# Attention with a gated spatial MLP on one core: f32 scores by 128 queries of one head with the two heads in row halves of the array, the last spatial block as two products, and new numbers for the plan

## Chip, core and metric

One NeuronCore of a Trainium2 chip runs the whole kernel. The metric is the device time of one execution in microseconds (us), median of the runs. Engine names: PE is the matrix engine, PEld its weight loads, DVE, ACT and POOL the three elementwise engines, SP the queue that issues the DMAs. A tile name like `ps` stands for any of its numbered buffers.

## What is computed

```python
def _attn_ref(q, k, v):                       # (4 batches, 12 heads, 448, 64)
    scores = scale * np.matmul(q, k.transpose(0, 1, 3, 2))
    scores = np.where(np.triu(ones, k=1), -1000000000.0, scores)
    scores = scores - np.max(scores, axis=-1, keepdims=True)
    attn = np.exp(scores)
    attn = attn / (np.sum(attn, axis=-1, keepdims=True) + 1e-09)
    return np.matmul(attn, v)
...
def _moe_ref(x, w_in, w_spatial, b_spatial, w_out):   # x: (4, 448, 768)
    h = np.maximum(x @ w_in, 0.0)                     # 768 -> 1024
    u, v = h[..., :512], h[..., 512:]
    v_n = (v - mean(v)) / np.sqrt(var(v) + 1e-06)
    v_s = np.einsum('ts,bsd->btd', w_spatial, v_n) + b_spatial[None, :, None]
    return (u * v_s) @ w_out                          # 512 -> 768
```

## The kernel before

The 48 heads are worked on as 24 pairs (6 to a batch). A pair goes through load of q and k, `qk_turn` or `qk_prepare` (transposed q and k in `qkT`), `attend` (scores, mask and maximum, exponential, division, transposed weights in `et`, product with v in `px`) and ends in `xT`, one sixth of a batch's feature rows split in an f16 high and low part. After a batch's pairs `ffn(b)` makes four groups of chained products in three PSUM banks `pf`: the v half (`wi` streamed, `xT` as weights), the u half (`xT` streamed), the spatial product (`wst` streamed, the normalised `vn` as weights) and the output (`wo` streamed, `g` and `gt` as weights). An f16 product is three matmuls, high by high, high by low, low by high (`TERMS`).

Pairs are treated in three ways. `SINGLE` (0 to 14): scores are one f32 product each. 64 queries of both heads stand as one block-diagonal weight tile (`q32`, 128 rows by 128 columns: head 0 in rows 0 to 63, head 1 in 64 to 127, zeros elsewhere), and k of both heads streams past it (`k32`); a unit `c` covers queries 64c to 64c+63 and streams 64(c+1) columns, seven units to a pair, two in a bank (`BANKS`). An f32 matmul stands in the trace as two records with a weight load each. The remaining pairs have their scores as f16 high and low products in column halves of the array (L746, L747) from q and k that DMAs transpose. `TURNED` (0 to 8): the weights after the softmax stay f32 and PE transposes them (L807), and the product with v (L893) is f32, one head in each column half of the array. The other pairs split them in f16 high and low and let DMAs transpose them.

Order: every function only adds operations with engines, estimated costs and dependencies to a `Plan`. `assign` spreads the free ones over ACT, DVE and POOL; `run` plays the estimates forward and fixes each engine's order and the buffers. `TUNE`, `SLACK`, `EARLY`, `SPLITS`, `LAZY` and the costs therefore decide where an operation stands, not what it does. For the four `ffn` groups and the pairs that means that PE's queue mixes chains of three (`pf`, L1118) with pieces of attention. Lines of the profile that are used: L578 transposes of q and k, L736 f32 scores, L746/L747 f16 scores, L757 mask and maximum, L769 exponential, L782/L790 division, L427/L459 and L438 high and low parts, L893 product with v, L1118 all `ffn` chains.

## Time and profile before

| | |
|---|---|
| median of 3 runs (range) | 406.49 us (405.89 to 406.72) |
| the profiled execution | 406.36 us, span 404.6 us |
| busy: PE, DVE, ACT, POOL | 371.9, 280.7, 259.2, 198.1 us |
| PE idle | 32.7 us of the span |

The span runs from the first to the last instruction; 1.8 us of the execution lie around it. Busy PE counts pipelined matmuls, so the price of a piece of PE work is read below from the start of one group to the start of the next one on a full queue, not from the length of its records.

### The profile page before, as it was taken

Reading aid. Unit: us, or ns where it says so; the run is one execution under the profiler, and the core shown is the slowest. Engines: PE = TensorE matmul, PEld = TensorE weight load, DVE = VectorE, ACT = ScalarE, POOL = GpSimd, SP = SyncE. Lnnn points to the kernel's source line nnn. Section 1 sums busy time; section 2 is a strip of 40 time slices with the busy share of each in tenths; the row PEclk is TensorE's granted clock in tenths of the full one; section 3 lists DMA queues with packets and bytes.
Section 4 is the critical chain, followed back from the end, with each engine's and each line's share of the span. In section 5 each row is a group of like instructions: output and inputs, shape, how many; then the busy total and the mean of one; then the engine's idle time right before and its main releaser. Section 6 shows DMA issues by size and latency. Waiting matters only on the chain. (4 is left out here: it accounts for less than half of the span.)

```text
span 404.6 us, 7631 instructions
## 1 busy us (share of the span) xinstructions
PE 371.9 (92%) x2438; PEld 231.4 (57%) x2438; DVE 280.7 (69%) x955; ACT 259.2 (64%) x744; POOL 198.1 (49%) x276
## 2 busy tenths in 40 slices
PE   5578869997999999999999999999996999999995
PEld 4455444663556466865545459855452568445595
DVE  4366868889767997977887898676996884031211
ACT  3779867688977566997867957666763655123120
POOL 2310489566887665006289387525892340054120
PEclk9899998999999999999999999999996999999999
DMA  8974882346193349997979978998775546400013
GB/s 176 235 154 145 222 170 101 105 95 148 43 219 87 118 123 172 172 226 174 192 161 206 169 135 191 190 208 197 128 137 105 98 87 120 129 2 0 0 48 109
DMA packets 156298, 55.60 MB, mean 137 GB/s; under 512 B 150177, under 2 KB 152034, under 8 KB 156258
## 3 DMA queue, kind: packets, MB, share of 16 engines
q1 hardware_dynamic: 156258, 55.12, 65.0%
q8 instruction: 19, 0.31, 0.3%
q14 instruction: 21, 0.17, 0.1%
HBM read 26.76 MB, written 5.51 MB: 80 GB/s over the span
## 5 line engine op out<-in xcount | busy, mean ns | idle before, releaser
L736 PE MATMUL ps<-qkT 128*128 128x64 f32 (+6 forms) x210 | 61.7, 422 | 6.8 <-ACT et L827 3.4
L769 ACT ACTIVATE ps<-ps,sm 128x384 f32<-128x384 f32 (+4 forms) x105 | 48.7, 464 | 29.6 <-DVE sm L757 21.6
L1118 PE MATMUL pf<-xT,wi 128*128 128x448 f16 x288 | 62.9, 356 | 0.2 <-ACT u L1265 0.2
L1118 PE MATMUL pf<-wi,xT 128*128 128x512 f16 (+1 forms) x360 | 62.3, 340 | 0.0
L1118 PE MATMUL pf<-wo,g 128*128 128x384 f32 x288 | 59.3, 351 | 0.2 <-DVE u L1291 0.2
L857 DVE SCALAR_TENSOR_TENSOR e<-ps,sm,e 128x256 f16<-128x256 f32 (+4 forms) x105 | 49.4, 504 | 9.4 <-ACT e L425 8.7
L427 POOL TENSOR_SCALAR e<-e,sm 128x64 f32<-128x64 f32 (+6 forms) x51 | 31.1, 626 | 49.4 <-DVE sm L790 33.8
L757 DVE CUSTOM_DVE_ANT_0 ps<-ps,mask 128x384 f32<-128x384 f32 (+6 forms) x105 | 44.1, 443 | 15.5 <-PE ps L736 14.7
L425 ACT ACTIVATE e<-ps,sm 128x384 f16<-128x384 f32 (+4 forms) x105 | 46.2, 507 | 13.3 <-DVE sm L790 9.5
L1118 PEld LDWEIGHTS pf<-wo,g 128*128 128x128 f32 x288 | 49.7, 188 | 4.6 <-issue 2.7
L1118 PE MATMUL pf<-wst,vn 128*128 128x448 f16 (+1 forms) x192 | 42.8, 364 | 4.4 <-ACT u L1265 3.8
L1118 PEld LDWEIGHTS <-xT 128*128 128x128 f16 (+1 forms) x360 | 26.4, 103 | 32.6 <-issue 11.9
L736 PEld LDWEIGHTS ps<-qkT 128*128 128x128 f32 x210 | 33.0, 199 | 16.3 <-ACT et L827 5.1
L1118 PEld LDWEIGHTS <-wi 128*128 128x128 f16 x288 | 26.0, 98 | 27.4 <-issue 7.5
L782 DVE TENSOR_SCALAR sm<-sm 128x2 f32<-128x2 f32 x96 | 24.1, 263 | 20.1 <-ACT e L769 10.4
L769 ACT ACTIVATE e<-ps,sm 128x384 f32<-128x384 f32 (+6 forms) x63 | 29.2, 476 | 11.7 <-DVE sm L757 10.0
L757 DVE CUSTOM_DVE_ANT_0 ps<-ps,mask,sc 128x384 f32<-128x384 f32 (+4 forms) x63 | 30.8, 504 | 4.4 <-PE ps L747 3.7
L427 POOL TENSOR_SCALAR vs<-vnat,vsc 128x512 f16<-128x512 f32 x15 | 10.5, 701 | 45.7 <-PE px L893 41.1
L1118 PEld LDWEIGHTS <-vn 128*128 128x128 f16 (+1 forms) x192 | 18.5, 100 | 23.7 <-issue 9.5
L807 PE MATMUL ps<-ident,e 128*128 128x128 f32 x144 | 22.1, 286 | 8.6 <-POOL e L427 5.2
L1211 POOL TENSOR_TENSOR ln<-ln,mhalf 128x1 f32<-128x1 f32 (+1 forms) x16 | 9.2, 581 | 36.7 <-DVE ln L1203 36.7
L807 PEld LDWEIGHTS ps<-ident,e 128*128 128x128 f32 x144 | 16.7, 145 | 17.2 <-POOL e L427 9.3
(122 smaller groups left out, 699.1 us busy)
## 6 DMA issues: line engine op xcount, KB each, us to landing
wb<-in_moe_w_in_dram SPq DMA_DIRECT2D x12, 512.0 KB, 4.0
vnat<-in_v_dram SPq DMA_DIRECT2D x24, 192.0 KB, 3.7
out_dram<-o SPq DMA_DIRECT2D x12, 384.0 KB, 3.3
qk<-in_q_dram SPq DMA_DIRECT2D x30, 112.0 KB, 3.7
qk<-in_k_dram SPq DMA_DIRECT2D x30, 112.0 KB, 3.7
o<-in_moe_w_out_dram SPq DMA_DIRECT2D x8, 384.0 KB, 3.4
qk<-in_q_dram SPq DMA_DIRECT2D x9, 224.0 KB, 3.8
qk<-in_k_dram SPq DMA_DIRECT2D x9, 224.0 KB, 4.3
```

The lines of the kernel that those rows point to most:

```text
L425: nc.scalar.activation(out=dst, in_=src, func=AF.Copy, scale=scale)
L427: nc.gpsimd.tensor_scalar(out=dst, in0=src, scalar1=scale, scalar2=1.0, op0=ALU.mult, op1=ALU.mult)
L736: nc.tensor.matmul(out=at(ps)[:, o0:o0 + n], lhsT=q32(t)[:, c, :], rhs=k32(t)[:, :n], start=True, stop=True)
L757: lambda e, ps=ps, n=n, u=u, sm=sm, o0=o0, m0=m0: nc.vector.tensor_tensor_reduce(out=at(ps)[:, o0:o0 + n], in0=at(ps)[:, o0:o0 + n], in1=m ...
L769: nc.scalar.activation(out=dst, in_=src, func=AF.Exp, scale=-1.0, bias=at(sm)[:, u:u + 1], accum_out=at(sm)[:, 4 + u:5 + u],)
L782: lambda e, n=n, sm=sm, esc=esc: nc.vector.tensor_scalar(out=at(sm)[:, 8:8 + n], in0=at(sm)[:, 4:4 + n], scalar1=1.0 / esc, scalar2=1e-9 / ...
L807: nc.tensor.transpose(out=at(pt)[:, 128 * i:128 * i + 128], in_=e32(at(eb))[:, E0[c] + j, :], identity=ident)
L857: lambda e, part=part, src=src, sm=sm, u=u: nc.vector.scalar_tensor_tensor(out=part(1), in0=src(), scalar=at(sm)[:, 8 + u:9 + u], in1=part(0),
L1118: nc.tensor.matmul(out=o, lhsT=a(), rhs=rhs, start=(n0 + n == 0), stop=(n0 + n == len(mms) - 1), skip_group_check=len(out_ap()) > 1,)
L1211: lambda e, ln=ln, tn=tn: nc.gpsimd.tensor_tensor(out=at(ln)[:tn, 8:9], in0=at(ln)[:tn, 8:9], in1=mhalf[:tn], op=ALU.pow),
```

## The change

1. Pairs that are both `TURNED` and `SINGLE` (now 0 to 9) are `WIDE`. A product takes 128 queries of one head: weights 64 rows by 128 columns, head 0 in rows 0 to 63, head 1 in rows 64 to 127 (`flat32`), and the two heads' products follow each other into different PSUM banks. Queries 0 to 127 stream 128 columns, 128 to 255 stream 256, 256 to 383 stream 384. The last 64 queries of both heads go to one bank, head 0 in partitions 0 to 63, head 1 in 64 to 127, each streaming 448. Three PE operations make a pair: `both(0)`, `both(2)`, `last()`. Mask, exponential, division and transposes follow the new grouping (`mask2`; five score banks to a pair where there were four, three groups of divisions where there were four).
2. `TURNED` gains pair 9; `SINGLE` loses pairs 12 to 14, which are now split and transposed like 15 to 23.
3. In the spatial product the last block of 64 tokens has its high part in rows 0 to 63 and its low part in rows 64 to 127, so that one matmul makes high by high and low by high. A second one makes high by low and the bias (`wst` and `vn3` are laid out for it, with one more copy per batch). Twelve matmuls of a chain become eleven.
4. The plan's numbers are new, so all engines' orders are.

```diff
 LAZY = 13750
 CALM = 5
-SPLITS = 1, 6
-EARLY = 20570
+SPLITS = 2, 7
+EARLY = 14463
 WAYS = "qkw"
 
-TURNED = frozenset(range(9))
-
-SINGLE = frozenset(range(15))
-SLACK = 345.0, 270.0, 0.0, 100.0, 412.0, 440.0
-TUNE = 23000.0, 5468.0, 44064.0, 3408.0, 785.0, 805.0, 3458.0, 21900.0, 6260.0, 15846.0
+TURNED = frozenset(range(10))
+
+SINGLE = frozenset(range(12))
+SLACK = 393.0, 184.0, 100.0, 40.0, 677.0, 440.0
+TUNE = 33297.0, 2734.0, 63857.0, 6028.0, 898.0, 884.0, 3458.0, 18815.0, 8564.0, 15846.0
 
 
 class Buf:
@@ -307,6 +308,8 @@
...
+
+    WIDE = [t and w for t, w in zip(TURNS, WHOLE)]
...
+
+    mask2 = phys["e"][0][:, 17 * 128:21 * 128]
...
-    store("sm", 3, [128, 16], F32)
+    store("sm", 6, [128, 16], F32)
...
-        if any(WHOLE):
-            for t in phys["qkT"]:
-                nc.vector.memset(q32(t), 0.0)
...
         t = s["qkT"] = Buf("qkT")
+        if not WIDE[p]:
...
-            parts = [(slice(0, 64), 0), (slice(64, 128), 64)] if n == 0 else [(slice(0, 128), None)]
+            parts = [(slice(0, 64), 0), (slice(64, 128), 64)] if n == 0 and not WIDE[p] else [(slice(0, 128), None)]
...
 
+
+
+    GROUPS = [
+        [(0, 0, 128, 0, 0), (0, 128, 256, 128, 1)],
+        [(1, 0, 128, 0, 3), (1, 128, 256, 128, 4)],
+        [(0, 256, 384, 0, 6)],
+        [(1, 256, 384, 0, 9)],
+        [(None, 384, S, 0, 12)],
+    ]
+    HR = 1408
+
+    def wide(p, eb, et):
+
+
+        s, rank = st[p], 100 * p
+        banks = [Buf("ps") for _ in GROUPS]
+
+        def product(h, q0, n, bank, o0, r0, rn):
+            t = at(s["qkT"])
+            rows = slice(64 * h, 64 * h + 64)
+            nc.tensor.matmul(
+                out=at(bank)[r0:r0 + rn, o0:o0 + n], lhsT=flat32(t)[rows, q0:q0 + rn], rhs=k32(t)[rows, :n],
+                start=True, stop=True, skip_group_check=True,
...
+        def both(g):
+            for i in range(len(GROUPS[g])):
+                for h in range(2):
+                    _, q0, n, o0, _ = GROUPS[g + h][i]
+                    product(h, q0, n, banks[g + h], o0, 0, 128)
+
+        def last():
+            for h in range(2):
+                product(h, 384, S, banks[4], 0, 64 * h, 64)
+
+        sums = [Buf("sm") for _ in range(3)]
+        whose = [(sums[g // 2], 2 * (g % 2) if g < 2 else g % 2) for g in range(5)]
+        for n, fn in enumerate((lambda e: both(0), lambda e: both(2), lambda e: last())):
+            parts = [(banks[g], u) for g in (2 * n, 2 * n + 1) if g < 5 for u in range(len(GROUPS[g]))]
+            plan.add({"PE": WIDE_PE[n]}, fn, s["qkT_keys"], parts + [(eb, "room")], rank)
...
+        for g, (ps, group) in enumerate(zip(banks, GROUPS)):
+            sm, u0 = whose[g]
+            for u, (h, q0, n, o0, _) in enumerate(group):
+                plan.add(
+                    {"DVE": c_dve(n) + 8},
+                    lambda e, ps=ps, n=n, u=u0 + u, sm=sm, o0=o0, h=h: nc.vector.tensor_tensor_reduce(
+                        out=at(ps)[:, o0:o0 + n], in0=at(ps)[:, o0:o0 + n],
+                        in1=mask[:, 0:n] if h is None else mask2[:, 512 - n:512],
+                        scale=-0.125, scalar=3.0e38, op0=ALU.add, op1=ALU.min, accum_out=at(sm)[:, u:u + 1],
+                    ),
+                    [const_key("mask")], [(ps, u), (sm, f"m{u0 + u}")], rank,
+                )
...
+        for n, sm in enumerate(sums):
+            m = (4, 2, 1)[n]
+            plan.add(
+                {"DVE": 250},
+                lambda e, m=m, sm=sm: nc.vector.tensor_scalar(
+                    out=at(sm)[:, 8:8 + m], in0=at(sm)[:, 4:4 + m], scalar1=1.0, scalar2=1e-9, op0=ALU.mult, op1=ALU.add,
+                ),
+                [(sm, f"s{u}") for u in range(m)], [(sm, "d")], rank,
+            )
...
+            def turn(e, pt=pt, c0=c0, cn=cn):
+                for i in range(cn):
+                    nc.tensor.transpose(
+                        out=at(pt)[:, 128 * i:128 * i + 128], in_=e32(at(eb))[:, c0 + i, :], identity=ident
+                    )
+
+            plan.add(
+                {"PE": cn * 116}, turn, [(eb, x[4]) for x in group] + [(eb, "pad"), const_key("ident")], [(pt, 0)],
+                rank, 200,
+            )
...
+            for i in range(2 if g < 2 else 1):
+
+                def copy(e, pt=pt, i=i, g=g):
+                    by_head = at(et).rearrange("p (h r) -> p h r", h=2)
+                    blocks = at(pt)[:, 0:384].rearrange("p (j r) -> p j r", r=128)
+                    if g < 2:
+
+                        src, dst = at(pt)[:, 0:256], by_head[:, g, 0:256]
+                        if i:
+                            src, dst = at(pt)[:, 256:384], by_head[:, g, 448:576]
+                    elif g < 4:
+                        src = blocks
+                        dst = by_head[:, g - 2, 256:256 + 960].rearrange("p (j r) -> p j r", r=320)[:, :, 0:128]
+                    else:
+                        src = at(pt).rearrange("p (j h r) -> p j h r", j=4, h=2)
+                        dst = by_head[:, :, 128:HR].rearrange("p h (j r) -> p j h r", r=320)[:, :, :, 256:320]
...
-        for g, units in enumerate(BANKS):
+        if WIDE[p]:
+            wide(p, eb, et)
+        for g, units in enumerate(() if WIDE[p] else BANKS):
...
+                            if WIDE[p]:
+                                rhs = at(et)[:kk, 1408 * h + 448 * j:1408 * h + 320 * j + S]
...
+            {"POOL": c_pool(S), "ACT": c_act(S)},
+            lambda e: scaled_copy(e, wst[64:128, 0, 3, :], wst[0:64, 0, 3, :], 1.0), [], [const_key("wst", 0)], rank + 2,
+        )
...
+            for plane in range(1 if t < 3 else 2):
+                plan.add(
+                    {"ACT": c_act(512), "POOL": c_pool(512), "DVE": c_fast(512)},
+                    lambda e, hv=hv, nb=nb, tn=tn, plane=plane: scaled_copy(e, at(nb)[:tn, plane], at(hv)[:tn], 1.0),
+                    [(hv, 0)], [(nb, "h" if not plane else "hh")], -1,
+                )
...
-                    out=at(nb)[:tn, 1], in0=at(hv)[:tn], in1=at(nb)[:tn, 0], op=ALU.subtract
+                    out=at(nb)[:tn, 1] if tn == 128 else at(nb)[64:128, 0], in0=at(hv)[:tn], in1=at(nb)[:tn, 0],
+                    op=ALU.subtract
                 ),
...
-                    for j, kk in enumerate((128, 128, 128, 65)) for a, w in TERMS
+                    for j in range(3) for kk in (128,) for a, w in TERMS
+                ] + [
+                    (
+                        lambda a=a, f=f, kk=kk: at(vn[3])[:kk, a, 128 * f:128 * f + 128],
+                        lambda a=a, kk=kk: [wst[:kk, a, 3, :]], [(vn[3], x) for x in xs] + [const_key("wst", a)],
+                    )
+                    for a, kk, xs in ((0, 128, "hl"), (1, 97, ("hh",)))
                 ],
```

PE around a pair's f32 scores, before (pair 8; `ps` score banks, `e` softmax weights, `pf` an ffn chain):

```order
L807 MATMUL ps1_73<-ident_64,e1_93 128x128 x4
L736 MATMUL ps2_74<-qkT0_84 128x64
L736 MATMUL ps2_74<-qkT0_84 128x384
L807 MATMUL ps3_75<-ident_64,e1_93 128x128 x4
L807 MATMUL ps1_73<-ident_64,e0_92 128x128 x4
L1118 LDWEIGHTS vn1_115
L1118 MATMUL pf2_79<-wst_65,vn1_115 128x448
```

PE around a pair's f32 scores, after (pair 9):

```order
L754 MATMUL ps0_72<-qkT1_85 128x128
L754 MATMUL ps2_74<-qkT1_85 128x128
L754 MATMUL ps0_72<-qkT1_85 128x256
L754 MATMUL ps2_74<-qkT1_85 128x256
L1288 LDWEIGHTS wi_63
L1288 MATMUL pf1_78<-xT4_100,wi_63 128x448
L1288 LDWEIGHTS wi_63
L1288 MATMUL pf1_78<-xT4_100,wi_63 128x448
L1288 LDWEIGHTS wi_63
L1288 MATMUL pf1_78<-xT4_100,wi_63 128x448
L754 MATMUL ps1_73<-qkT1_85 128x384
L754 MATMUL ps3_75<-qkT1_85 128x384
```

The scores of a pair still stand in pieces among chains of three; a piece is now two or four matmuls with 64 weight rows, and matmuls with 128 rows stand before and behind it. Counted over the whole of PE's order, the array's tile shape (rows by columns of weights) differs from one matmul to the next at 155 places before and at 210 after; 53 of these have a wide product on one side.

PE at the end of a spatial chain of batch 0, before:

```order
L736 MATMUL ps1_73<-qkT1_85 128x256 x2
L1118 LDWEIGHTS vn3_66
L1118 MATMUL pf2_79<-wst_65,vn3_66 128x448
L1118 LDWEIGHTS vn3_66
L1118 MATMUL pf2_79<-wst_65,vn3_66 128x448
L1118 LDWEIGHTS vn3_66
L1118 MATMUL pf2_79<-wst_65,vn3_66 128x448
```

and after:

```order
L1288 LDWEIGHTS wi_63
L1288 MATMUL pf2_79<-xT5_101,wi_63 128x448
L1288 LDWEIGHTS vn3_66
L1288 MATMUL pf1_78<-wst_65,vn3_66 128x448
L1288 LDWEIGHTS vn3_66
L1288 MATMUL pf1_78<-wst_65,vn3_66 128x448
L1288 LDWEIGHTS wi_63
```

The block `vn3` has two matmuls where it had three.

POOL between the normalisation of batch 2 and its gates, before (`qk` and `qks` are the high and low parts of a pair's q and k, `vs` those of its v):

```order
L427 TENSOR_SCALAR vn3_66<-hv1_113 64x512
L427 TENSOR_SCALAR qk2_82<-qk2_82,sc2_122 112x512
L1242 TENSOR_TENSOR vn3_66<-hv1_113,vn3_66 64x512
L427 TENSOR_SCALAR qk2_82<-qk2_82,sc2_122 112x512
L427 TENSOR_SCALAR qks0_83<-qk2_82 112x8x64 x2
L459 TENSOR_TENSOR qks0_83<-qk2_82,qks0_83 112x8x64 x2
L427 TENSOR_SCALAR vs0_90<-vnat1_87,vsc1_126 128x8x64
L427 TENSOR_SCALAR vs1_91<-vnat1_87,vsc1_126 128x8x64
L427 TENSOR_SCALAR g0_105<-u0_104 128x384
```

and after:

```order
L1413 TENSOR_TENSOR vn2_116<-hv0_112,vn2_116 128x512
L1413 TENSOR_TENSOR vn3_66<-hv1_113,vn3_66 64x512
L436 TENSOR_SCALAR vn3_66<-hv1_113 64x512
L436 TENSOR_SCALAR vs1_91<-vnat1_87,vsc1_129 128x8x64
L436 TENSOR_SCALAR qk2_82<-qk2_82,sc2_125 112x512 x2
L436 TENSOR_SCALAR qks0_83<-qk2_82 112x8x64 x2
L468 TENSOR_TENSOR qks0_83<-qk2_82,qks0_83 112x8x64 x2
L436 TENSOR_SCALAR g0_105<-u0_104 128x384
```

The run of six operations on `qk2` and `qks` stands there again, now wholly behind `vn3` and with `vs1` ahead of it. On DVE the subtraction for `vs` stands right behind the scale of that same pair in both orders.

## Rows read from the trace of the kernel before

**Rows 1.** The page: span, then busy time, share and instructions of each engine.

```profile
span 404.6 us, 7631 instructions
PE 371.9 (92%) x2438; PEld 231.4 (57%) x2438; DVE 280.7 (69%) x955; ACT 259.2 (64%) x744; POOL 198.1 (49%) x276
```

**Rows 2.** Four stretches: busy time of PE, PEld, DVE, ACT, POOL; granted clock, DMA share, GB/s.

```profile
0.00:62.00 62.00, 43.93 (x238) 28.56 (x238) 37.24 (x154) 45.53 (x135) 21.82 (x50) 0.97 0.83 180
62.00:304.00 242.00, 235.65 (x1618) 144.00 (x1618) 204.18 (x690) 178.83 (x526) 151.09 (x195) 0.99 0.75 155
304.00:314.00 10.00, 6.24 (x25) 2.14 (x23) 6.51 (x17) 4.02 (x10) 2.02 (x3) 0.66 0.54 96
314.00:400.30 86.30, 86.09 (x564) 56.67 (x562) 32.74 (x96) 30.33 (x74) 23.19 (x30) 1.00 0.28 65
```

**Rows 3.** Timeline of PE, 115 to 146 us: start, length, group, count.

```profile
115.17 2.10 PE L893 MATMUL px<-et,vnat 128*64 128x448 f32 x16
117.20 1.89 PE L736 MATMUL ps<-qkT 128*128 128x192 f32 x8
...
128.13 1.03 PE L736 MATMUL ps<-qkT 128*128 128x64 f32 x4
129.00 1.04 PE L807 MATMUL ps<-ident,e 128*128 128x128 f32 x8
129.88 0.73 PE L1118 MATMUL pf<-wst,vn 128*128 128x448 f16 x3
...
139.74 0.92 PE L736 MATMUL ps<-qkT 128*128 128x448 f32 x2
140.50 3.57 PE L1118 MATMUL pf<-wst,vn 128*128 128x448 f16 x18
143.90 0.55 PE L578 MATMUL ps<-ident,qk 112*128 112x112 f32 x4
144.29 1.87 PE L1118 MATMUL pf<-wst,vn 65*128 65x448 f16 x9
```

**Rows 4.** Timeline of PE, 105 to 107 us: half and full array in turn.

```profile
105.28 0.52 PE L1118 MATMUL pf<-wi,xT 128*64 128x256 f16 x6
105.73 0.74 PE L1118 MATMUL pf<-xT,wi 128*128 128x448 f16 x3
106.40 0.52 PE L1118 MATMUL pf<-wi,xT 128*64 128x256 f16 x6
```

**Rows 5.** Timeline of PE, 252 to 257 us: f16 product with v, then f16 scores.

```profile
252.01 1.62 PE L893 MATMUL px<-et,vs 128*64 128x448 f16 x24
253.56 0.28 PE L746 MATMUL ps<-qkT 128*64 128x192 f16 x2
...
255.00 0.80 PE L1118 MATMUL pf<-wo,g 128*128 128x384 f32 x3
255.73 0.38 PE L746 MATMUL ps<-qkT 128*64 128x448 f16 x2
...
256.23 2.87 PE L1118 MATMUL pf<-wo,g 128*128 128x384 f32 x15
```

**Rows 6.** The chain that ended last, from 300 us: start, length, what.

```profile
300.54 1.42 DVE sc L479
301.97 4.59 DVE vs L438
...
307.47 0.64 ACT u L1265
...
308.15 4.64 PE pf L1118 x12
```

**Rows 7.** Timeline of POOL beside it.

```profile
301.26 0.68 POOL L427 TENSOR_SCALAR qk<-qk,sc 112x512 f32<-112x512 f32 x1
...
305.33 0.69 POOL L427 TENSOR_SCALAR vs<-vnat,vsc 128x512 f16<-128x512 f32 x1
```

**Rows 8.** The group of that DVE line: count, busy us, mean ns, idle before.

```profile
L438 DVE SCALAR_TENSOR_TENSOR vs<-vnat,vsc,vs 128x512 f16<-128x512 f32 x15 | 16.3, 1086 | 0.5 <-POOL vs L427 0.4
```

More of the change, by code (lines that the diff above doesn't have):

```diff
@@ L341, in q32, with flat32 @@
         return t.bitcast(F32)[:, 0:2 * S].rearrange("p (c r) -> p c r", r=128)
+    def flat32(t):
+        return t.bitcast(F32)[:, 0:S]
     def k32(t):
@@ L528, in constants @@
         nc.gpsimd.memset(mask[:, S:512], NEG)
+        nc.gpsimd.memset(mask2[:, 0:384], 0.0)
+        nc.gpsimd.memset(mask2[:, 384:512], 0.0)
+        nc.gpsimd.affine_select(
+            out=mask2[:, 384:512], in_=mask2[:, 384:512], pattern=[[-1, 128]], compare_op=ALU.is_ge, fill=NEG,
+            base=0, channel_multiplier=1,
+        )
         for t in phys["e"]:
@@ L565, in load @@
             )
+    blank = {}
     def qk_turn(p):
@@ L571, in qk_turn, with clear @@
         t = s["qkT"] = Buf("qkT")
+        if not WIDE[p]:
+            def clear(e):
+                if not blank.get(at(t).name):
+                    nc.gpsimd.memset(q32(at(t)), 0.0)
+                    blank[at(t).name] = True
+            plan.add({"POOL": 300}, clear, [], [(t, (0, 0)), (t, (0, 1))], rank)
         for n in range(2):
@@ L585, in qk_turn, with copy @@
             )
-            parts = [(slice(0, 64), 0), (slice(64, 128), 64)] if n == 0 else [(slice(0, 128), None)]
+            parts = [(slice(0, 64), 0), (slice(64, 128), 64)] if n == 0 and not WIDE[p] else [(slice(0, 128), None)]
             for i, (rows, c0) in enumerate(parts):
-                def copy(e, pt=pt, rows=rows, c0=c0):
+                def copy(e, pt=pt, rows=rows, c0=c0, n=n):
                     src = at(pt)[rows, :S]
                     if c0 is None:
-                        dst = k32(at(t))
+                        dst = k32(at(t)) if n else flat32(at(t))
+                        if not n:
+                            blank[at(t).name] = False
                     else:
@@ L700, with even @@
     held = {}
+    GROUPS = [
[41 more added lines that the diff above has]
+                )
+            for u, (_, _, n, o0, c) in enumerate(group):
+                plan.add(
+                    {"ACT": c_act(n, "P", 2)},
+                    lambda e, ps=ps, n=n, u=u0 + u, sm=sm, o0=o0, c=c: nc.scalar.activation(
+                        out=at(eb)[:, 128 * c:128 * c + n], in_=at(ps)[:, o0:o0 + n], func=AF.Exp, scale=-1.0,
+                        bias=at(sm)[:, u:u + 1], accum_out=at(sm)[:, 4 + u:5 + u],
+                    ),
+                    [(sm, f"m{u0 + v}") for v in range(len(group))], [(ps, u), (sm, f"s{u0 + u}"), (eb, c)], rank,
+                )
[5 more added lines that the diff above has]
+                    out=at(sm)[:, 8:8 + m], in0=at(sm)[:, 4:4 + m], scalar1=1.0, scalar2=1e-9, op0=ALU.mult, op1=ALU.add,
+                ),
+                [(sm, f"s{u}") for u in range(m)], [(sm, "d")], rank,
+            )
+            plan.add(
+                {"DVE": 150},
+                lambda e, m=m, sm=sm: nc.vector.reciprocal(out=at(sm)[:, 8:8 + m], in_=at(sm)[:, 8:8 + m]),
+                [], [(sm, "d")], rank,
+            )
+        for g, group in enumerate(GROUPS):
+            sm, u0 = whose[g]
+            for u, (_, _, n, _, c) in enumerate(group, u0):
+                def even(e, c=c, u=u, sm=sm, n=n):
+                    w = at(eb)[:, 128 * c:128 * c + n]
+                    scaled_copy(e, w, w, at(sm)[:, 8 + u:9 + u])
+                plan.add(
+                    {"POOL": 260 + 1.25 * n, "ACT": c_act(n, "S", 1), "DVE": c_fast(n, 1)}, even, [(sm, "d")],
+                    [(eb, c)], rank,
+                )
+            pt = Buf("ps")
+            c0, cn = group[0][4], 4 if g == 4 else 3
+            def turn(e, pt=pt, c0=c0, cn=cn):
+                for i in range(cn):
+                    nc.tensor.transpose(
+                        out=at(pt)[:, 128 * i:128 * i + 128], in_=e32(at(eb))[:, c0 + i, :], identity=ident
+                    )
+            plan.add(
+                {"PE": cn * 116}, turn, [(eb, x[4]) for x in group] + [(eb, "pad"), const_key("ident")], [(pt, 0)],
+                rank, 200,
+            )
+            for i in range(2 if g < 2 else 1):
[12 more added lines that the diff above has]
+                        dst = by_head[:, :, 128:HR].rearrange("p h (j r) -> p j h r", r=320)[:, :, :, 256:320]
+                    if e == "ACT":
+                        nc.scalar.activation(out=dst, in_=src, func=AF.Copy)
+                    else:
+                        nc.vector.tensor_copy(out=dst, in_=src)
+                n = (256, 128)[i] if g < 2 else 128 * cn
+                plan.add({"ACT": c_act(n, "P"), "DVE": c_dve(n)}, copy, [(pt, 0)], [(et, (g, i))], rank)
@@ L862, in attend @@
                 )
-        if turns:
+        if WIDE[p]:
+            et_keys = [(et, (g, i)) for g in range(5) for i in ((0, 1) if g < 2 else (0,))]
+        elif turns:
             et_keys = [(et, (g, i)) for g in range(4) for i in ((0, 1) if g == 1 else (0,))]
```

44 lines of the change are left out of this document (26 added, 18 removed).

## Prediction

> **What bounds the kernel now.** I read the page first, then busy time by stretches, then PE's timeline, last the chain that ended last. The page says that PE is busy 371.9 of 404.6 us and no other engine more than 280.7 [rows 1]. The stretches say where the 32.7 us of idle PE lie: 18.1 in the first 62 us, 6.3 in the next 242, 3.8 in the 10 us from 304, 0.2 in the 86 after that, and 4.3 behind PE's last matmul [rows 1, 2]. So from 62 us on PE has a full queue but for one hole, and what leaves its queue there shortens the kernel, while in the first 62 us PE waits for the other engines and work taken from it mostly becomes idle time. DVE is next, 84 % busy from 62 to 304 us, ACT 74 %, POOL 62 % [rows 2]. The chain shows what the hole is: a subtraction for `vs` on DVE that holds the chain 4.59 us, then an ACT evacuation, then PE starts again at 308.15 [rows 6].
>
> **Prices on PE.** Start to start on a full queue: 18 matmuls of 448 f16 columns take 3.40 us, 0.189 each, 0.42 ns a column [rows 3]. The f32 unit of 448 columns takes 0.76 us (139.74 to 140.50), 1.70 ns a column, four passes of the f16 price; the units of 64 and 384 together 0.87 (128.13 to 129.00), 0.11 above their columns, so a short unit pays a floor [rows 3]. A pair of 0 to 8 has 1792 columns: 0.87 + 0.76 + 896 × 1.70 ns = 3.15 us. For pairs 9 to 14 the program widens odd units, 1920 columns, 3.37 us.
>
> The f32 product with v puts one head into each column half. Its 2 × 1024 columns would take 3.48 us one after the other; they take 2.03 (115.17 to 117.20), so halves of the array do run side by side in f32, at 1.74 plus 0.29 [rows 3]. That is column halves; no row shows row halves.
>
> What entering and leaving a half costs is read where six half matmuls of 256 f16 columns alternate with three full ones: 0.45 and 0.67 us [rows 4]. Two at a time, six would take 0.32; three full ones take 0.57. That leaves 0.23 for two changes, 0.115 each.
>
> **The change, term by term.**
> 1. *Scores in row halves.* A head streams 128 + 256, then 384, then 448 columns; side by side 1216 × 1.70 ns = 2.06 us a pair, one after the other 4.13. I take 2.06: the product with v is the nearest row, f32 in halves of the same array. Nine pairs gain 1.09 each and pair 9 gains 1.31: −11.1 us. The weight loads of the first operation are not known; a transpose shows 0.11 us per 128 columns of f32 weights (eight in 0.88, 129.00 to 129.88 [rows 3]), and eight loads that don't overlap would be 0.88 where the columns take 0.65. That is 0 to +2.3 us over ten pairs; I take 0 and keep the rest for the range.
> 2. *Changes of shape.* 210 instead of 155 in PE's order: 55 × 0.115 = +6.3 us. This eats more than half of term 1, because the pieces stand among full-array chains.
> 3. *Pairs 12 to 14 in f16.* Such a pair takes 1.44 + 0.50 us with its way out and 0.115 in [rows 5], 2.05 instead of 3.37: −4.0. Their 24 transposes of q and k go, four in 0.39 us (143.90 to 144.29 [rows 3]): −2.3. Three small sums come, no dearer than a transpose: +0.3.
> 4. *Pair 9 by PE.* Sixteen transposes at 0.11: +1.8. The product with v is 2.03 us in f32 instead of 1.55 in f16 (252.01 to 253.56) [rows 3, 5]: +0.5.
> 5. *Spatial block.* Sixteen matmuls fewer at 0.189: −3.0.
> 6. *Other engines and DMAs.* Counted in the order, DVE has 20 instructions fewer, ACT 9 more, POOL 36 more. Their cover is the idle 16, 26 and 38 % of the second stretch [rows 2]; a microsecond more on ACT is paid by nobody. DMAs: three transposes and six local copies come for pairs 12 to 14, their q and k come in six loads instead of twelve, three transposes of pair 9's weights go; SP issues as many as before, and the DMA share of 0.75 [rows 2] is its cover. Without cover a pair would wait for its `qkT`; I take nothing.
>
> Terms 1 to 5: −11.1 + 6.3 − 4.0 − 2.3 + 0.3 + 2.3 − 3.0 = −11.5 us of PE work.
>
> 7. *Early pairs.* Pairs 0 to 3 are scored before 62 us. Their net gain, 1.09 less about 0.63 for changes of shape, I don't count: +1.8.
> 8. *The hole at 304 us.* DVE's subtraction starts behind the 1.42 us of L479 and lasts until POOL's six operations on `qk`, `qks` and `vs`, back to back from 301.26 to 306.02, are over [rows 6, 7]; DVE is queued, ACT's evacuation behind it, PE behind that. The loss is 3.8 us idle, and a granted clock of 0.66 (1.2 GHz for two thirds of the window, the rest at 2.4) after the pause [rows 2]; about 6.5 us together. In the changed order POOL's run and DVE's subtraction stand as close as before. But the 15 such subtractions average 1.09 us [rows 8], so mostly they don't meet a run. Between 0 and 6.5 I credit half: −3.3.
>
> Sum: −11.5 + 1.8 − 3.3 = −13.0 on the span, 404.6 to 391.6, 393.4 us with the 1.8 around it. The profiled execution is 0.1 under the median of the three runs, so **393.5 us**.
>
> A rule of the Trainium skill speaks against term 1: TensorEngine Tiling (Array Packing), Gotcha 1: PSUM Pressure, says that different row tiles cannot use one PSUM bank at a time. `last()` writes one bank from both row halves. In the product with v two halves write one bank at once without paying for it [rows 3], but those are column halves; by the rule the sum would come out as in rival B.
>
> **Rivals.**
> A. *The hole stays, or moves.* New order, same neighbours on POOL and DVE. If it costs the whole 6.5, the time is 396.8; with a second one of its size, 403.3. For it: POOL gets busier by three pairs' high and low parts, six operations each, nearly 5 us (five take 4.07 in the run of [rows 7]). Against it: one such hole in 400 us so far.
> B. *`last()` runs one head after the other.* Ten times 0.76: +7.6, 401.1 us. For it, only the shared bank; against it, that its two heads also lie in different columns of the array, as in the product with v.
> C. *Row halves don't run side by side at all* (the other sign). A pair then takes 4.13 us, 2.07 more: ten pairs +20.7, and +12.4 if the four early ones stay hidden: 406 to 414, I say 411. It decides from about 3.4 us a pair, where the 13.0 are used up. For it: no row shows row halves, and f32 takes two records and two loads for each product. Against it: column halves do it in f32.
> D. *More than the sum.* The hole goes wholly (−3.3) and the early gain counts (−1.8): 388.4.
>
> On C the skill's page TensorE: Matmul & The Clock Gate, Part 3, states that matmuls in distinct row groups run concurrently (4 row strips measured at 3.07 times the speed); no row here shows it, and by it the sum is that of term 1.
>
> **How the numbers follow.** A run here tells about 0.2 % from no change, 0.8 us. Chances: forecast 48 %, A 23 %, B 8 %, C 9 %, D 12 %. The range 387 to 402 us leaves out C, the end of A with two holes and the far end of D, about 2 in 10; it holds the 2.3 us of weight loads. The likeliest case by itself reaches from 390 to 396.5. Faster: all but C and a sliver of A, 0.89; within 0.2 %: 0.02; slower: 0.09.
>
> **What will show it.** In the timeline of the changed kernel: `last()` at 0.76 us and `both(2)` at 0.65, start to start, plus about 0.1 at either end (B would show 1.5 for the first, C 1.3 for the second too); eleven matmuls in a spatial chain at 0.189; PE busy near 360 us; L746/L747's successors for 12 pairs; and in the stretches no 10 us at a clock of 0.66. The forecast is wrong if a change of shape costs an f32 product with fresh weights much more than 0.115 us, if the first 62 us lengthen because the new order starts the weights' preparation later, or if DVE, at 84 %, becomes what PE waits for.

## The result and the profile after

| | before | after |
|---|---|---|
| median (range) | 406.61 us (405.89 to 406.88, 4 runs) | 391.76 us (389.81 to 393.82, 4 runs) |
| the profiled execution, span | 406.36, 404.6 us | 389.81, 388.1 us |
| PE busy, PE idle | 371.9, 32.7 us | 359.0, 29.1 us |

The ratio is 0.9651, 95 % interval 0.9615 to 0.9687. The runs of after spread over 1 %, four times as far as those of before; the profiled execution is the fastest of the four. Executions over 1.5 % above the fastest of their kernel are left out below (three of ten of the kernel with all pairs in the same rows, two of six of that with the early four, one of six of that with pairs 12 to 14 in f32), but for one kernel whose six runs are all told.

The page of after, the lines that answer to [rows 1]:

```profile
span 388.1 us, 7762 instructions
PE 359.0 (93%) x2474; PEld 216.7 (56%) x2474; DVE 276.5 (71%) x935; ACT 252.1 (65%) x759; POOL 225.2 (58%) x312
```

The stretches of after, columns as in [rows 2]: PE, PEld, DVE, ACT, POOL, granted clock, DMA share, GB/s.

```profile
0.00:62.00 62.00, 49.80 (x301) 27.80 (x301) 39.23 (x162) 50.94 (x164) 27.73 (x62) 0.97 0.83 187
62.00:290.00 228.00, 215.98 (x1561) 128.43 (x1561) 195.57 (x646) 164.48 (x500) 166.62 (x213) 0.99 0.79 163
290.00:300.00 10.00, 10.00 (x64) 5.04 (x64) 8.55 (x31) 6.52 (x21) 7.45 (x9) 1.00 0.63 123
300.00:384.00 84.00, 83.26 (x554) 55.41 (x550) 33.12 (x99) 29.94 (x77) 23.39 (x30) 1.00 0.33 75
```

PE's idle time is 12.2 us in the first 62 us (18.1 before), 12.0 in the next 228 (6.3 before in the 242 us up to the hole), none around 300 us, 0.7 until 384 and 4.1 behind PE's last matmul. So the hole is gone, the beginning is fuller, and the middle has become emptier.

The timeline of PE in after, the pieces of a wide pair (L754) and what follows each:

```profile
112.22 0.97 PE L754 MATMUL ps<-qkT 64*64 64x448 f32 x4
113.11 0.55 PE L826 MATMUL ps<-ident,e 128*128 128x128 f32 x3
...
117.56 0.93 PE L754 MATMUL ps<-qkT 64*128 64x128 f32 x8
118.42 0.74 PE L1288 MATMUL pf<-xT,wi 128*128 128x448 f16 x3
119.09 0.92 PE L754 MATMUL ps<-qkT 64*128 64x384 f32 x4
119.94 1.88 PE L1288 MATMUL pf<-xT,wi 128*128 128x448 f16 x9
121.96 0.97 PE L754 MATMUL ps<-qkT 64*64 64x448 f32 x4
122.86 1.14 PE L898 MATMUL ps<-qkT 128*128 128x64 f32 x4
```

Start to start `both(0)` takes 0.86 us, `both(2)` 0.85, `last()` 0.89 and 0.90: 2.60 us a pair, its changes of shape included, where the block-diagonal tile took 3.15.

The subtractions for `vs` on DVE in after (count, then min/median/max in ns), to be read against [rows 8]:

```profile
L447 DVE SCALAR_TENSOR_TENSOR vs<-vnat,vsc,vs x14: 741/744/1196, 84.3 to 317.2; 128x512 f16<-128x512 f32 x14
```

None of the 14 is stretched beyond 1.2 us, where one of 15 took 4.69 (4.59 of it in the chain of [rows 6]).

### The profile page after: what moved, and what is told of

It reads as the page before. It is cut to its first block, busy times and chain, and to the rows that moved or that the text cites. A ratio compares the mean times of both kernels' runs of the same rounds, so it can differ in the third digit from the quotient of the medians.

```text
span 388.1 us, 7762 instructions
## 1 busy us (share of the span) xinstructions
PE 359.0 (93%) x2474; PEld 216.7 (56%) x2474; DVE 276.5 (71%) x935; ACT 252.1 (65%) x759; POOL 225.2 (58%) x312
## 5 line engine op out<-in xcount | busy, mean ns | idle before, releaser
L436 POOL TENSOR_SCALAR e<-e,sm 128x128 f32<-128x128 f32 (+3 forms) x54 | 31.3, 595 | 35.6 <-DVE sm L806 21.1
L1288 PEld LDWEIGHTS <-xT 128*128 128x128 f16 (+1 forms) x360 | 26.1, 103 | 31.1 <-issue 11.5
L434 ACT ACTIVATE e<-ps,sm 128x384 f16<-128x384 f32 (+4 forms) x98 | 41.0, 520 | 3.6 <-DVE sm L952 3.6
L919 DVE CUSTOM_DVE_ANT_0 ps<-ps,mask,sc 128x256 f32<-128x256 f32 (+4 forms) x84 | 39.0, 506 | 4.6 <-PE ps L909 4.2
L789 ACT ACTIVATE e<-ps,sm 128x128 f32<-128x128 f32 (+3 forms) x70 | 34.3, 503 | 7.2 <-DVE sm L779 5.0
L754 PE MATMUL ps<-qkT 64*128 64x128 f32 (+3 forms) x160 | 30.4, 459 | 4.0 <-ACT e L789 3.2
L779 DVE CUSTOM_DVE_ANT_0 ps<-ps,e 128x256 f32<-128x256 f32 (+2 forms) x60 | 24.1, 442 | 7.1 <-PE ps L754 6.7
L468 POOL TENSOR_TENSOR qks<-qk,qks 112x512 f16<-112x512 f32 x24 | 29.1, 1229 | 0.0
L851 ACT ACTIVATE et<-ps 128x256 f32<-128x256 f32 (+3 forms) x64 | 23.4, 437 | 5.3 <-PE ps L826 3.6
L1288 PEld LDWEIGHTS <-vn 128*128 128x128 f16 (+1 forms) x176 | 16.5, 99 | 17.7 <-issue 4.5
L436 POOL TENSOR_SCALAR qk<-qk,sc 112x512 f32<-112x512 f32 x24 | 16.9, 715 | 15.5 <-ACT ps L931 8.7
L1059 PE MATMUL px<-et,vs 128*64 128x448 f16 (+3 forms) x336 | 22.7, 276 | 2.6 <-DMA et<-e 1.5
```

The costliest lines, as they stand in the source:

```text
L434: nc.scalar.activation(out=dst, in_=src, func=AF.Copy, scale=scale)
L436: nc.gpsimd.tensor_scalar(out=dst, in0=src, scalar1=scale, scalar2=1.0, op0=ALU.mult, op1=ALU.mult)
L468: lambda e: HANDLE[e].tensor_tensor(out=dst_l(), in0=src(), in1=dst_h(), op=ALU.subtract),
L754: nc.tensor.matmul(out=at(bank)[r0:r0 + rn, o0:o0 + n], lhsT=flat32(t)[rows, q0:q0 + rn], rhs=k32(t)[rows, :n], start=True, stop=True, ski ...
L779: lambda e, ps=ps, n=n, u=u0 + u, sm=sm, o0=o0, h=h: nc.vector.tensor_tensor_reduce(out=at(ps)[:, o0:o0 + n], in0=at(ps)[:, o0:o0 + n], in ...
L789: lambda e, ps=ps, n=n, u=u0 + u, sm=sm, o0=o0, c=c: nc.scalar.activation(out=at(eb)[:, 128 * c:128 * c + n], in_=at(ps)[:, o0:o0 + n], fu ...
```

## The experiments

Where an edit changes the engines' orders, it is said; the others keep them. Times are medians; the change is against the 391.76 us of after, unless before is named; ratios are to runs of before on the same chip, whose medians were 405.8 to 406.4 us. In kernels of the same order an ACT instruction can be looked up in both traces; the difference of its two starts is called the lag behind after. Some 2 us of it belong to the profiled execution of after: the four kernels of its order whose edit comes later lag by 1.7 to 2.8 us at 15 us already. What sets them apart is the first clock record of the trace, at 9.6 us in after and at 14.7 to 16.9 us in these four; what it means is read below.

**Side by side, all ten pairs, then the late six, then the early four.**

```diff
-            rows = slice(64 * h, 64 * h + 64)
+            rows = slice(0, 64)
```

> The changed kernel with both heads' products in rows 0 to 63 of the array; the order on every engine, the columns streamed and the shapes stay. Head 1 is scored with head 0's q and k, so that half of the scores of pairs 0 to 9 is not computed. Theory (the gain comes from two row halves that stream at the same time): both(0) and both(2) go from 0.86 and 0.85 us, start to start, to about 1.50, 0.65 more each; last() stays at 0.89, because its two heads still lie in different column halves; PE busy rises by about 13 us, and the time by 7.8 (pairs 4 to 9 only) to 13 us, to 400 to 405 us. Rival 1 (the gain comes from larger products, with fewer loads and records, not from side by side): both pieces stay under 1.0 us and the time moves by less than 2 us. Rival 2 (it takes different rows as well as different columns): last() goes to 1.65 too, and the time to 405 to 412 us.

Measured 401.64 us (400.37 to 403.18), +9.9, ratio 0.9901 (0.9876 to 0.9925): the theory's size. Where the 9.9 us are lost isn't read from this kernel's trace: that execution took 408.3 us, with a granted clock of 0.50, which is 1.2 GHz, from 33.6 to 47.2 and from 54.0 to 64.3 us. The two kernels that follow tell it.

```diff
+            rows = slice(64 * h, 64 * h + 64) if p < 4 else slice(0, 64)
```

> The changed kernel with both heads' products in rows 0 to 63 for pairs 4 to 9 alone; the order stays. Head 1 of these pairs is scored with head 0's q and k. Theory (read from the run with all ten pairs so: in the changed kernel the stretch from 62 to 170 us is bound by other engines, mostly DVE, and the early pairs carry the gain): six pairs take 1.3 us of PE more each, 7.8 in all, but the time rises by less than 2.5 us, and PE's idle time between 62 and 170 us falls by 5 us or more. Rival (as forecast: the pairs after 62 us are on the path and the first four are not): up by 6 to 9 us.

The timeline of PE in this kernel, the pieces of pair 9 which the timeline of after above has from 117.56 to 122.86 us:

```profile
121.84 1.57 PE L754 MATMUL ps<-qkT 64*128 64x128 f32 x8
123.35 0.74 PE L1288 MATMUL pf<-xT,wi 128*128 128x448 f16 x3
124.02 1.55 PE L754 MATMUL ps<-qkT 64*128 64x384 f32 x4
125.51 1.88 PE L1288 MATMUL pf<-xT,wi 128*128 128x448 f16 x9
127.31 0.97 PE L754 MATMUL ps<-qkT 64*64 64x448 f32 x4
128.22 1.14 PE L898 MATMUL ps<-qkT 128*128 128x64 f32 x4
```

Start to start `both(0)` takes 1.51 us instead of 0.86 and `both(2)` 1.49 instead of 0.85, while `last()` stays at 0.91. Columns, shapes and neighbours are the same, so the 0.65 us are the two row halves' running at the same time; `last()`, whose heads lie in different column halves as well, doesn't need different rows. Rivals 1 and 2 of the run with all ten pairs fall with this.

Measured 395.21 us (393.65 to 396.46), +3.4, ratio 0.9730 (0.9698 to 0.9762). Of 7.8 us of work about half or less reaches the end (the spread of both kernels leaves some 1 to 5 us); this lies between the theory's 2.5 and the rival's 6. The stretch from 62 to 170 us, first of after, then of this kernel:

```profile
62.00:170.00 108.00, 98.42 (x627) 57.73 (x627) 97.59 (x292) 80.58 (x242) 86.34 (x109) 0.98 0.62 139
```

```profile
62.00:170.00 108.00, 101.04 (x618) 59.00 (x618) 95.45 (x285) 79.21 (x237) 87.11 (x110) 1.00 0.59 133
```

PE's idle time there falls from 9.6 to 7.0 us, not by the 5 us expected.

```diff
+            rows = slice(64 * h, 64 * h + 64) if p > 3 else slice(0, 64)
```

> The changed kernel with both heads' products in rows 0 to 63 for pairs 0 to 3 alone; the order stays. Head 1 of these pairs is scored with head 0's q and k. Theory (the first pairs stand on the path, because ACT and DVE wait for PE's scores there): the ten pairs together cost 10.9 us, pairs 4 to 9 alone 3.4 us, so 7.5 us by difference, up by 6 to 10 us to 398 to 402 us, with the loss made before 62 us. Rival (as forecast: what PE does for these pairs is hidden in its idle time before 62 us): up by less than 2 us, and the loss of the run with ten pairs came from late pairs after all, through the order in which stalls meet.

Measured 397.36 us (396.58 to 399.58), +5.6, ratio 0.9802 (0.9769 to 0.9835); the rival falls. The theory's 6 is just missed. The lag is 8.2 us at 22 us already, 9.2 at 57 and 8.6 at 206: pairs 0 and 1 make nearly all of it. Early on everything on PE is slower. The timeline of PE in after:

```profile
8.66 1.01 PE L603 MATMUL ps<-ident,qk 112*128 112x112 f32 x4
9.60 1.61 PE L754 MATMUL ps<-qkT 64*128 64x384 f32 x4
...
13.32 0.60 PE L603 MATMUL ps<-ident,qk 112*128 112x112 f32 x4
```

and of this kernel:

```profile
10.30 1.01 PE L603 MATMUL ps<-ident,qk 112*128 112x112 f32 x4
11.23 7.47 PE L754 MATMUL ps<-qkT 64*128 64x384 f32 x16
18.63 1.01 PE L603 MATMUL ps<-ident,qk 112*128 112x112 f32 x4
...
32.16 0.60 PE L603 MATMUL ps<-ident,qk 112*128 112x112 f32 x4 [1.60 <-DVE et L853]
```

Four transposes of q and k take 1.01 us at 8.66 and 0.60 at 13.32 in after, and here 1.01 still at 18.63 and 0.60 at 32.16; a `both(2)` takes 1.61 at 9.60 where it takes 0.92 later. The windows before 25 us read a granted clock of 1.00 in both kernels, but that is no reading: the traces hold no record of the clock before 9.62 us in after and before 28.02 us here, and a window without a record is printed as 1.00. What PE's clock was there is told by its own operations, beside a stretch of the kernel with late rows that has records:

```profile
26.00:32.00 6.00, 5.43 (x22) 3.63 (x24) 1.89 (x9) 5.60 (x19) 0.00 (x0) 0.50 0.97 247
```

```profile
26.46 1.01 PE L603 MATMUL ps<-ident,qk 112*128 112x112 f32 x4 [2.41 <-DVE et L853]
```

At 0.50, 1.2 GHz, the four transposes take the same 1.01 us. And in each of the fourteen traces PE's operations become nearly twice as fast where the first record stands. So PE starts at 1.2 GHz, and the doubled products of pairs 0 and 1 are paid at nearly twice their later price. The rise stands at 26.7 and 28.0 us in the two kernels that give up the row halves early, and between 9.6 and 18.4 us in the twelve others, so the edit itself seems to put it off, although PE is busy here without a pause from 10.30 us on. Only two traces say so, and how much of the 5.6 us is the later rise wasn't separated.

Why PE's speed counts there is told by what DVE waits for in the first 30 us, in before, in after and in this kernel (total, times, longest):

```profile
DVE ps L757 <- PE ps L736: 11.1, 2, 5.9
```

```profile
DVE ps L779 <- PE ps L754: 5.2, 4, 4.5
```

```profile
DVE ps L779 <- PE ps L754: 12.3, 9, 5.3
```

**What PE waits for between 62 and 170 us.**

```diff
-                from_double(w, raw, hc, [(rb, 0)], (tb, 1), rank)
+                from_double(lambda w=w: w()[:, 0:16], lambda raw=raw: raw()[:, 0:16], hc, [(rb, 0)], (tb, 1), rank)
```

> The changed kernel with DVE's 24 operations that unpack w_out from doubles cut from 384 columns to 16, so that most of w_out is not read; the order stays. They stand between 62 and 170 us and take some 16 us of DVE. Theory (DVE, nearly 10 of 10 us busy from 90 to 170 us, is what PE waits for there): PE's idle time from 62 to 170 us falls by 4 us or more, and the time by 4 to 8 us, to 384 to 388 us. Rival 1 (PE's waits there are the latency of a pair's chain through ACT): less than 1.5 us. Rival 2 (time won there is lost again on a later wait, before 290 us): a gain at 170 us that is gone at 290 us.

Measured 387.49 us (386.62 to 388.05), −4.3, ratio 0.9540 (0.9512 to 0.9568). The same stretch:

```profile
62.00:170.00 108.00, 101.66 (x647) 59.95 (x646) 92.24 (x309) 83.74 (x255) 86.64 (x115) 0.98 0.68 145
```

PE is idle 6.3 us there instead of 9.6, and the lag goes from +2.7 us at 61 us to −2.0 at 159, and is −1.8 at 345. What is won there isn't lost later. DVE's unpacking of w_out is on the path. Whether by DVE's own queue alone isn't separated: POOL's operations beside it also became shorter (23 on `e` 0.60 us each instead of 0.64).

**The hole of before.**

```diff
-        t = Buf("qks")
+        t, w = Buf("qks"), 2 if p == 23 else 64
...
-                "qk"[n], lambda n=n: at(t)[:, n, :, 0:64], lambda n=n: at(t)[:, n, :, 64:128], lambda n=n: at(s["qk"])[:, n],
+                "qk"[n], lambda n=n: at(t)[:, n, :, 0:w], lambda n=n: at(t)[:, n, :, 64:64 + w], lambda n=n: at(s["qk"])[:, n, :, 0:w],
```

> The kernel before, in its own order, with the six operations on q and k of pair 23 (scale, high and low part, all on POOL around 300 to 305 us) cut to 2 of 64 columns, so that pair 23's q and k are left unscaled and unsplit for the most part. Theory (the hole at 304 us comes from DVE's subtraction for vs, stretched to 4.69 us by POOL's run beside it): the subtraction takes 0.75 to 1.2 us, PE has no hole between 304 and 308 us and keeps its full clock there, and the time falls by 4 to 6.5 us, to 400 to 402.5 us. Rival 1 (the hole is 3.8 us of idle time alone, and the low clock in that stretch comes from elsewhere): 3 to 4 us. Rival 2 (the subtraction is slow for another reason, or another wait ends at the same time): within 1 us.

Measured 400.96 us (399.52 to 401.47), 5.4 under before, ratio 0.9862 (0.9840 to 0.9885). The timeline of DVE in this kernel, where [rows 6] had 4.59 us:

```profile
302.15 0.48 DVE L479 TENSOR_SCALAR sc<-sc 128x2 int32<-128x2 int32 x1
302.54 0.76 DVE L438 SCALAR_TENSOR_TENSOR vs<-vnat,vsc,vs 128x512 f16<-128x512 f32 x1
```

and its stretch from 304 us, with PE full and the clock at 1.00:

```profile
304.00:314.00 10.00, 10.00 (x86) 5.09 (x84) 7.88 (x25) 6.98 (x20) 1.60 (x3) 1.00 0.61 122
```

The theory holds: POOL's run makes the hole. By the medians it was worth 5.4 us. In the traces this kernel lags before by 1.7 us at 290 us, nearly all of it from before 62 us, and leads it by 4.9 at 320: 6.6 us at the hole itself, which is the 6.5 of idle time and clock taken together.

**Twelve matmuls in a spatial chain.** The first form let the planner see the twelfth, which changed the order on every engine; its expectation took the order to stay, and that was wrong.

```diff
-                    for a, kk, xs in ((0, 128, "hl"), (1, 97, ("hh",)))
+                    for a, kk, xs in ((0, 128, "hl"), (1, 97, ("hh",)), (1, 97, ("hh",)))
```

> The changed kernel with the eleventh matmul of each spatial chain issued a second time, so that the chain has twelve again; the order stays. The repeated product is counted twice in the result. Theory (a matmul on PE's full queue costs its 0.189 us, so the fifth term was worth 3.0 us): PE busy up by 3.0 us, time up by 2.5 to 3.5 us. Rival (the spatial chains run where PE has slack, waiting for DVE's and POOL's work on v): less than 1 us.

Measured 408.48 us (407.15 to 410.60), +16.7, ratio 1.0067 (1.0043 to 1.0092), for 3.0 us of matmuls. The second form holds the order:

```diff
-                    for o, rhs in zip(out_ap(), w()):
+                    for o, rhs in list(zip(out_ap(), w())) * (2 if len(mms) == 11 and n0 + n == 9 else 1):
```

> The changed kernel with the tenth matmul of each spatial chain issued twice inside one planned operation, at the cost that the planner had for one, so that every engine's order stays. The repeated product counts twice in the result. Theory (a matmul on PE's path costs its 0.189 us, and the 16.7 us of the run with twelve planned matmuls came from another order): time up by 2.2 to 3.5 us. Rival 1 (the spatial chains are where PE is waited for by all, and a longer one sets off waits on DVE): up by more than 8 us, as in the run with twelve planned ones. Rival 2 (it is hidden): under 1 us.

Measured 400.18 us, the median of all six runs: five at 399.1 to 402.5 and one at 394.15. The lag is some 1.4 us until 186 us, 2.5 to 3.3 between 206 and 216, and 7.7 to 9.5 from 222 us on. Between the last two stands this on DVE:

```profile
216.75 4.58 DVE L488 TENSOR_SCALAR sc<-sc 128x2 int32<-128x2 int32 x1
```

and on POOL in the same kernel:

```profile
215.88 1.35 POOL L436 TENSOR_SCALAR qk<-qk,sc 112x512 f32<-112x512 f32 x2
217.21 1.20 POOL L436 TENSOR_SCALAR qks<-qk 112x512 f16<-112x512 f32 x2
218.38 2.25 POOL L468 TENSOR_TENSOR qks<-qk,qks 112x512 f16<-112x512 f32 x2
220.62 0.69 POOL L436 TENSOR_SCALAR vs<-vnat,vsc 128x512 f16<-128x512 f32 x1
```

In after the same two stand like this, DVE first:

```profile
214.18 0.61 DVE L488 TENSOR_SCALAR sc<-sc 128x2 int32<-128x2 int32 x1
```

```profile
214.15 1.21 POOL L436 TENSOR_SCALAR qks<-qk 112x512 f16<-112x512 f32 x2
215.32 2.27 POOL L468 TENSOR_TENSOR qks<-qk,qks 112x512 f16<-112x512 f32 x2
```

An operation on 128 x 2 numbers takes 0.61 us in after and 4.58 here, and ends as POOL's run ends; the subtraction in before ended 0.5 us behind the end of its run. PE waits for what stands behind it, and the clock falls to 0.50, 1.2 GHz, from 222.9 to 226.3 us:

```profile
221.89 0.38 PE L513 MATMUL px<-vsc,ones 128*128 128x1 f32 x2 [3.25 <-DVE sm L944]
```

In after, too, the operation stands beside POOL's run, which goes there from 212.82 to 218.27 us, but it ends as a single POOL operation ends, at 214.8. Why it gets through there and not here, these runs don't show. The run at 394.15 us, +2.4, is what the theory says, with one run to show it; no trace of it was kept, so that it lacks the hole is inferred, from the time and from its mean granted clock, 0.991 where the other five have 0.979 to 0.986.

**The third and second part, by the planner's new order.** Both kernels have other orders than after.

```diff
-    WIDE = [t and w for t, w in zip(TURNS, WHOLE)]
+    WIDE = [False for t, w in zip(TURNS, WHOLE)]
```

> The changed kernel with no pair scored wide: pairs 0 to 9 as before in f32 by a block-diagonal tile, everything else as in the changed kernel; the planner makes a new order from the same numbers. Theory (a wide pair costs 2.60 us of PE with its changes of shape, measured, against 3.15 to 3.37): PE busy up by 4 to 6 us, and the time up by 3 to 6 us, to 395 to 398 us. Rival 1 (the row halves give nothing once the changes of shape are paid): PE busy and time within 1.5 us. Rival 2 (the numbers fit only the wide pairs): PE busy up by 4 to 6 us as in the theory, but idle time of PE grows by as much again or more, 400 us and over.

Measured 411.72 us (411.02 to 413.86), +20.0, ratio 1.0148 (1.0119 to 1.0177): rival 2 in time and idle time. PE is busy 370.3 us, 11.3 more, about twice what it said, and idle 41.2, 12.1 more; in the first 62 us it does 42.59 us of work, at a granted clock of 0.86, so part of the busy time is the clock. What the row halves alone are worth isn't read from this kernel.

```diff
-SINGLE = frozenset(range(12))
+SINGLE = frozenset(range(15))
```

> The changed kernel with pairs 12 to 14 scored in f32 by block-diagonal products again, not in f16; the planner makes a new order. Theory (the third term): PE busy up by 4.0 + 2.3 - 0.3 = 6.0 us, time up by 5 to 7 us, to 397 to 399 us. Rival (the work saved on PE is given back as waits for DMA transposes and the splits on POOL, so undoing it costs little): PE busy up by 6 us, but the time up by less than 3 us, with less idle time of PE between 150 and 290 us.

Measured 394.76 us (393.81 to 395.89; a sixth run took 888.34), +3.0, ratio 0.9724 (0.9700 to 0.9749), between the theory's 5 and the rival's 3. The page:

```profile
PE 367.4 (94%) x2450; PEld 223.7 (57%) x2450; DVE 273.5 (70%) x921; ACT 252.8 (64%) x755; POOL 209.5 (53%) x294
```

PE's busy time rises by 8.4 us, its idle time falls from 29.1 to 24.7. So half of what PE saves is given back as waits; in another order, this isn't the f16 pairs' doing alone.

**The plan's numbers.** In after those of before, and in before those of after:

```diff
-SPLITS = 2, 7
-EARLY = 14463
+SPLITS = 1, 6
+EARLY = 20570
...
-SLACK = 393.0, 184.0, 100.0, 40.0, 677.0, 440.0
-TUNE = 33297.0, 2734.0, 63857.0, 6028.0, 898.0, 884.0, 3458.0, 18815.0, 8564.0, 15846.0
+SLACK = 345.0, 270.0, 0.0, 100.0, 412.0, 440.0
+TUNE = 23000.0, 5468.0, 44064.0, 3408.0, 785.0, 805.0, 3458.0, 21900.0, 6260.0, 15846.0
```

> The changed kernel with the plan's numbers of the kernel before (SPLITS, EARLY, SLACK, TUNE), so in another order; what each operation does stays. Theory (the numbers carry the 3.6 us by which PE's idle time fell, above all the first 62 us, where it does 5.9 us more work): PE busy as in the changed kernel within 1.5 us, time up by 3 to 8 us, to 395 to 400 us, with idle time of PE in the first 62 us back near 18 us. Rival 1 (the numbers only undo what the new products disturbed): idle time grows by more than 10 us, 402 us and over. Rival 2 (the numbers do nothing): within 1.5 us.

> The kernel before with the new plan's numbers alone. Theory (the numbers carry the shorter idle time and move the hole at 304 us): PE busy stays at 372 within 1.5 us, PE's idle time falls by 3 to 6 us, and the time comes out at 400 to 404 us. Rival 1 (the numbers fit only the new products): slower than before, over 408 us. Rival 2: the same within 1 us.

| median, us | old numbers | new numbers |
|---|---|---|
| code of before | 406.4 | 414.87 (ratio 1.0212, 1.0187 to 1.0237) |
| code of after | 398.22 (ratio 0.9810, 0.9780 to 0.9840) | 391.76 |

The first kernel meets its theory in size (+6.5), less so in place: PE is idle 15.3 us before 62 us, not 18, and 31.9 in all. The second is slower, rival 1. The numbers alone cost 8.5 us, and with the new products they bring 6.5. In the trace of the code of after with the old numbers there is no hole: from 300 to 310 us PE is busy 10.00 us at a clock of 1.00, and no subtraction for `vs` takes more than 1.79 us.

**The price of a change of shape.**

```diff
+                        if len(mms) == 11 and n == 1 and n0 < 9:
+                            k = 128 if n0 == 3 else 64
+                            nc.tensor.matmul(
+                                out=o[:, 0:128], lhsT=ident[:k, :], rhs=ones[:k, :], start=False, stop=False,
+                                skip_group_check=True,
+                            )
```

> The changed kernel with an f32 product of 128 columns put into the middle of three of the four steps of each spatial chain: with 64 weight rows in the first and third step, with 128 rows (no change of shape) in the second. It adds the identity to the result. Read start to start on PE's timeline after 290 us. Theory (a change of shape costs about 0.115 us also where an f32 product with fresh weights follows): the step with 64 rows takes 0.2 to 0.25 us longer than the one with 128 rows. Rival 1 (shape costs nothing; the 0.2 us by which a wide piece exceeds its columns are its weight loads): both steps alike within 0.05 us. Rival 2: 0.4 us and more.

One run, 415.60 us. The timeline of PE in this kernel:

```profile
319.86 0.55 PE L1288 MATMUL pf<-wst,vn 128*128 128x448 f16 x2
320.35 0.49 PE L1294 MATMUL pf<-ones,ident 64*128 64x128 f32 x2
320.76 0.74 PE L1288 MATMUL pf<-wst,vn 128*128 128x448 f16 x3
...
327.59 0.74 PE L1288 MATMUL pf<-wst,vn 128*128 128x448 f16 x3
328.17 0.38 PE L1294 MATMUL pf<-ones,ident 128*128 128x128 f32 x2
328.38 0.35 PE L1288 MATMUL pf<-wst,vn 128*128 128x448 f16 x1
```

From 319.86 to 320.76 run two matmuls of 0.189 and the product with 64 rows: 0.52 us for it. From 327.59 to 328.38 run three and the one with 128 rows: 0.22. The difference, 0.30 us, is two changes, 0.15 each; at 321.44 and 323.86 the same sums give 0.51 and 0.23. Both rivals fall, and so does the theory's size, 0.2 to 0.25: here a change costs 0.15 us, a quarter to a third above the 0.115.

## Why the prediction was right, point by point

391.76 us against 393.5 forecast: right in size, and right that row halves run side by side and that the hole goes. But it is a sum in which steps failed with opposite signs, and that they cancel within 2 us is in part luck.

- **Terms 1 and 2** hold as prices. PE's busy time fell by 12.9 us, forecast 11.5. The two heads do run side by side: `both(2)` takes 0.85 us in two row halves and 1.49 in one. So they do in `last()` with its single bank: 0.89 us, where rival B asked for 1.5. Rival C falls with `both(2)` at 0.85. The rule of the Trainium skill, TensorEngine Tiling (Array Packing), Gotcha 1, which spoke for rival B, is not borne out by this trace for two 64 x 64 tiles in different rows and columns. The row groups at once that the Trainium skill, TensorE: Matmul & The Clock Gate, Part 3, states are shown here in f32, by the same 0.85 and 1.49 us. Term 2's price of 0.115 a change depends on the neighbours: it is 0.15 around the short product above, while the wide pieces exceed their columns by 0.21, 0.20 and 0.13 us, so at most 0.07 to 0.11 a change. Fifty-five changes are 4 to 8 us by these prices, and the 6.3 lies between.
- **Term 7**, "early pairs ... I don't count", failed. Giving up the row halves costs 5.6 us in the four early pairs, nearly all in pairs 0 and 1, and 3.4 in the late six. The step behind it, "from 62 us on PE has a full queue ... while in the first 62 us PE waits for the other engines", was read from busy shares. At the beginning DVE waits for PE's scores, 11.1 us of the first 30 in before, so PE is on the path there although it is idle for 18 of 62 us; and until 10 us or later it works at 1.2 GHz, where a piece costs nearly twice the price of the sum. From pair 2 on the term is nearer the truth: the lag grows by no more than 1 us between 22 and 57 us. What the change itself won there against the block-diagonal tiles wasn't measured by itself. A full PE of before was no sign of how near DVE stood, either: DVE was busy 93.5 of the 108 us from 62 to 170 already.
- **Term 6** failed in its cover: "the idle 16, 26 and 38 % of the second stretch". DVE is busy 97.6 of the 108 us from 62 to 170 in after, and taking most of 16.5 us of unpacking from it brings 4.3. This is the announced third sign, DVE as what PE waits for. How much of the forecast gain it ate wasn't measured by itself.
- **Term 3** gave half at the end: 3.0 us instead of 6.0, though PE's busy time moved by 8.4, in another order. **Term 5** is in keeping with the one run at +2.4; the traced run of that kernel meets a new hole, and the other four by their times probably do. **Term 4** wasn't tried by itself.
- **Term 8**, the hole, was right in mechanism and size (5.4 us by the medians, 6.6 by the traces, for 6.5), and "I credit half" was the wrong half: it went wholly. Rival A was no fancy, though: a collision of the same kind came back at 217 us when 0.19 us were added to a chain. In the traces of the two kernels with other products DVE operations beside POOL's took up to 3.17 us (at 218.7, without wide pairs) and 2.45 us (at 216.9, with pairs 12 to 14 in f32).
- **The sum.** The code with the old numbers gives 8.2 us, and the hole is gone in it already. With 5.4 to 6.6 us for the hole, terms 1 to 7 come to 2 to 3 us in that order instead of 9.7; this is an estimate, as the hole's price is that of the kernel before. The new numbers bring 6.5 us more, and these are not the hole's: they stood in no term. What they did is seen on ACT, which evacuates pair 3's product with v at 57.7 us in after, at 65.5 in before and at 65.5 in after's code with the old numbers; part of that may be the clock, whose first record stands at 9.6, 10.2 and 18.4 us. Why terms 1 to 7 came to so little in the old order stays open: PE is idle 31.9 us in that trace, where before has 28.9 outside its hole.

## What to carry over

Ask of each stretch which engine the others wait for, not which is busiest: extra work on PE was dear in the stretch where it was idle a fifth of the time, and about half free where it was nine tenths busy. A granted clock of 1.00 before the first clock record is no reading: look at how long a known operation takes. Hold the order when a single price is wanted; a change that the planner sees moves the whole program (16.7 us for 3.0 us of matmuls). Numbers tuned for one version of a program are part of that version: moved to the other they cost 8.5 us.
